# A float64 weight matrix read once, in column eighths, inside an attention loop

## The chip, the cores and the metric

The program runs on one core of one Trainium2 chip. The metric is the device time of one execution in microseconds, so lower is better; 0.3% of it is about 4.3 us.

## What is computed

Three stages follow each other: clustered attention, a feed-forward layer with a hard-swish in its middle, and a layer of eight experts with dense routing. The first matrix of the feed-forward layer is what the change is about.

```python
# q, k, v: 2 x 8 heads x 768 x 64; 16 centroids for each head; the weights come as float64
mask = q_assign[:, :, :, None] == k_assign[:, :, None, :]
scores = np.where(mask, scale * np.matmul(q, k.transpose(0, 1, 3, 2)), -1000000000.0)
attn = np.exp(scores - scores.max(-1)); attn = attn / (attn.sum(-1) + 1e-09)
x = np.matmul(attn, v)                       # to 1536 x 512
...
h = x @ w_in                                 # w_in: 512 x 2048
g = h * np.clip(h + 3.0, 0.0, 6.0) / 6.0
x = g @ w_out                                # w_out: 2048 x 512
...
out += P[:, e:e + 1] * (np.maximum(x @ w1[e], 0.0) @ w2[e])   # e = 0..7
```

## The kernel before

**The attention loop.** There are 16 heads of six blocks of 128 rows, 96 units in all. Unit g runs these steps, each for another block: `max_unit` for unit g + 8 (two small matmuls on TensorE, PE, into the one PSUM buffer `pmt`, L757; then VectorE, DVE, takes each row's maximum from it, L778), `s_mm` for unit g (eight matmuls into `pS`, L757), the exponential on ScalarE, ACT (`E`, L840), its float16 high part (`Eh`, L848) and the rest (`El`, on GpSimd, POOL, L857, or on DVE, L850), and `pv_mm` for unit g - 4 (L871). After a head's sixth maximum DVE writes the negated maxima as float16 terms to `nE` (L808 to L810), and SyncE, SP, turns them by a transposing DMA into `E` (L805). The last two matmuls of `pS` of the head's first unit need that `E`: the maxima of a head are ready at unit 6i - 2, and its first `pS` is at unit 6i.

**Preparation, beside the loop.** Heads go in pairs, counted from 0. For a pair, SP loads `qraw` and `kraw` (L477), the sum of squares goes over `red` to a scale (`qk_r`, L86, is DVE's maximum; a PE matmul, L91, spreads it to all rows), the float16 parts `nH` and `nL` are made (L624 for `nL`) and turned by transposing DMAs to `H` and `L` (L644). `sim` (PE, L655) compares with the centroids, a chain of DVE operations makes the argmax and the one-hot codes `a_oh` (L666 to L683), which a DMA turns into `ET` (L699). `abs4` (L742, L743) ends a small computation on the tile `ab`. When a head is done its output is scaled, split (`xn`, L909, POOL) and turned to `xT` (L911, SP).

**The first half of `w_in`** (512 x 1024 float64) is prepared by `first_weights` inside this loop. It goes over SP's queue twice. First, eight pieces of 512 KB (`w00x`) are read for their largest magnitude alone (L362, DVE), and one scale is made by `top_steps` (a matmul that turns the maxima, DVE's reduce, a matmul that spreads the result). Then eight column eighths of 512 KB (`w00f`, two buffers) are decoded from float64 to float32 by one ACT operation (L190) and four of DVE (L196, L198, L215, L217, `w00t`), and split into two float16 parts, `fhi` (L409, ACT) and `flo` (L412, DVE). The layer's PE work starts behind unit 95.

**What sets the order.** Everything is placed by hand: `at(unit, f)` puts a step into a unit, and tables of units (`PLACE`, `PLAN2`, `PLAN3`, `COLS`) name them; `PLAN2` holds pair 2, `PLAN3` pair 3. Each engine, and SP's queue, works in program order. A column's units in the table before are those of load, L190, the four DVE operations, `fhi` and `flo`:

```python
    COLS = [
        (44, 48, 49, 50, 61, 62, 64, 70), (45, 66, 71, 71, 72, 73, 74, 77),
        (63, 74, 78, 78, 79, 80, 81, 83), (74, 80, 84, 84, 85, 86, 87, 88),
    ] + [(u - 8, u, u + 1, u + 1, u + 2, u + 2, u + 3, u + 4) for u in (89, 95, 101, 107)]
```

Of the kernel before, what the change touches and what calls it, by code (L numbers as in the profile page):

```python
# [35 lines left out]
def attention_moe_kernel(  # L36
# [164 lines left out]

    def decode_max(m, nm):

        t = small.tile([P, 1], U32, tag="mt", name=f"{nm}_mt")
        tf = t.bitcast(F32)
        nc.vector.tensor_scalar(out=tf, in0=m, scalar1=F64_LEAST, scalar2=F64_MOST, op0=ALU.max, op1=ALU.min)
        nc.vector.tensor_scalar(
            out=t, in0=t, scalar1=5, scalar2=2, op0=ALU.logical_shift_left, op1=ALU.logical_shift_right)
        nc.vector.scalar_tensor_tensor(
            out=m.bitcast(U32), in0=m.bitcast(U32), scalar=0xC0000000, in1=t,  # L210
            op0=ALU.bitwise_and, op1=ALU.bitwise_or)
# [1749 lines left out]
```

## Time and profile before

| | us |
|---|---|
| median of 3 runs | 1437.73 (1434.11 to 1438.73) |
| the profiled execution | 1438.4, span 1436.6 |
| PE busy | 1357.0 of the span |
| DVE busy | 1169.0 |
| ACT busy | 936.9 |
| POOL busy | 839.6 |

The span is that of the profiled execution; about 1.8 us of its time lie around it. The loop's units can be found by ACT's `E` operation of each: unit 12 at 78.0 us, 24 at 106.9, 36 at 135.5, 48 at 162.7, 60 at 189.8, 72 at 221.0, 84 at 247.6 and 95 at 272.0. A busy share is a mean over the attention loop and the two layers behind it, so the rows below are read by stretch. The brackets at the end of a row of an engine's timeline give the idle time before the instruction and what ended it.

### The profile page before, as it was taken

How to read it: one execution, taken by the hardware profiler on the slowest of the kernel's cores; microseconds unless marked ns; L12 is line 12 of the kernel's file. 1: busy time of each engine (PE TensorE's matmuls, PEld its weight loads, DVE VectorE, ACT ScalarE, POOL GpSimd, SP SyncE). 2: the span in 40 equal slices, each digit the busy share in tenths (PEclk: the TensorE clock that was granted, in tenths of full speed). 3: DMA queues.
4: the chain of work that ended last, by engine and by line, in shares of the span. 5: the costliest groups of instructions: out<-in, count | busy, mean ns of one | idle time of the engine just before them, and what ended most of it. 6: DMA issues, size and time to landing. Idle time of an engine off the chain costs nothing.

```text
span 1436.6 us, 32199 instructions
## 1 busy us (share of the span) xinstructions
PE 1357.0 (94%) x12855; PEld 1049.8 (73%) x12855; DVE 1169.0 (81%) x2059; ACT 936.9 (65%) x1760; POOL 839.6 (58%) x889
## 2 busy tenths in 40 slices
PE   5779888899999988999999999999999999999998
PEld 2456655544444447878888888888888888888887
DVE  7688889677766579978997998988988988988864
ACT  5689988675563637587676566566666666656642
POOL 2588888453134448497575476466566566666631
PEclk9799999999999999999999999999999999999999
DMA  6367533323311100110201211211101111111001
GB/s 199 88 146 125 111 71 62 97 91 91 118 60 32 60 1 17 47 38 24 60 32 31 60 31 31 60 31 32 57 20 46 45 32 46 45 31 46 9 30 52
DMA packets 141399, 82.90 MB, mean 58 GB/s; under 512 B 77760, under 2 KB 137152, under 8 KB 141248
## 3 DMA queue, kind: packets, MB, share of 16 engines
q1 hardware_dynamic: 141104, 80.81, 21.3%
q8 instruction: 100, 1.64, 0.5%
q14 instruction: 51, 0.42, 0.1%
q10 hardware_dynamic: 144, 0.03, 0.0%
HBM read 64.01 MB, written 3.15 MB: 47 GB/s over the span
## 4 chain that ended last, share of the span: by engine, by line
PE 64%; DVE 18%; ACT 5%; issue 4%; POOL 4%; DMA 3%; SPq 0%; DVEq 0%; POOLq 0%; ACTq 0%
PE o_X L1771 16%; PE X L1830 16%; PE o_Z L1771 8%; PE Z L1830 8%; PE Y L1830 4%; PE o_Y L1771 4%; DVE pmt L778 4%; PE pmt L757 2%; PE pS L757 2%; PE l L1389 2%; PE pv L871 1%; DMA E<-nE 1%; DVE raw L217 1%; DVE w_t L215 1%; ACT u L1359 1%
## 5 line engine op out<-in xcount | busy, mean ns | idle before, releaser
L1830 PEld LDWEIGHTS <-wop 128*128 128x128 f16 x4032 | 394.5, 98 | 66.0 <-issue 19.1
L1771 PEld LDWEIGHTS <-g 128*128 128x128 f16 x4032 | 394.3, 98 | 46.0 <-DVE g L1735 0.4
L1771 PE MATMUL o_X<-ws,g 128*128 128x256 f16 x2304 | 312.1, 273 | 0.1
L1735 DVE TENSOR_TENSOR g<-xT,g 128x512 f16<-128x512 f32 (+1 forms) x288 | 233.6, 811 | 1.1 <-ACT g L1730 0.9
L1739 POOL TENSOR_TENSOR xT<-xT 128x256 f32<-128x256 f32 x96 | 79.3, 826 | 264.7 <-ACT xT L1841 263.9
L1830 PE MATMUL X<-xop,wop 128*128 128x256 f16 x1536 | 210.0, 274 | 11.3 <-DVE xT L1838 6.7
L857 POOL TENSOR_TENSOR El<-E,Eh 128x384 f16<-128x384 f32 x162 | 161.6, 1024 | 56.6 <-ACT Eh L848 29.5
L1730 ACT CAST g<-xT 128x512 f16<-128x512 f32 (+1 forms) x288 | 157.8, 548 | 7.4 <-POOL xT L1743 7.3
L1771 PE MATMUL o_Z<-ws,g 128*128 128x256 f16 x1152 | 156.1, 273 | 0.0
L1835 ACT COPY xT<-X 128x256 f32<-128x256 f32 x192 | 71.0, 370 | 129.4 <-PE X L1830 129.2
L1367 POOL TENSOR_TENSOR hl<-u,hh 128x512 f16<-128x512 f32 x48 | 62.1, 1294 | 88.8 <-ACT hh L1366 88.8
L1841 ACT ACTIVATE xT<-xT 128x256 f32<-128x256 f32 x192 | 100.0, 521 | 18.2 <-DVE xT L1838 17.6
L840 ACT ACTIVATE E<-pS,esc 128x768 f32<-128x768 f32 x96 | 86.4, 900 | 39.0 <-PE pS L757 28.0
L1830 PE MATMUL Z<-xop,wop 128*128 128x256 f16 x768 | 104.8, 273 | 2.6 <-ACT xT L1835 2.6
L1841 ACT ACTIVATE xT<-X 128x256 f32<-128x256 f32 x96 | 36.7, 382 | 105.1 <-PE X L1830 104.9
L1830 PE MATMUL X<-xT,wop 128*128 128x256 f16 x768 | 104.7, 273 | 0.4 <-ACT xT L1835 0.3
L1800 DVE SCALAR_TENSOR_TENSOR acc<-o_X,coef,acc 128x256 f32<-128x256 f32 x168 | 73.0, 474 | 28.0 <-PE o_X L1771 28.0
L1744 POOL TENSOR_TENSOR sb<-xT 128x256 f32<-128x256 f32 x96 | 89.4, 931 | 7.5
L1743 POOL TENSOR_TENSOR xT<-xT 128x256 f32<-128x256 f32 x96 | 92.4, 962 | 0.0
L778 DVE TENSOR_REDUCE pmt<-pmt 128x2 f32<-128x768 f32 x84 | 80.7, 960 | 12.2 <-PE pmt L757 11.2
L1740 POOL TENSOR_TENSOR sb<-xT 128x256 f32<-128x256 f32 x96 | 82.1, 855 | 6.4 <-ACT xT L1835 3.6
L1838 DVE TENSOR_TENSOR xT<-X,xT 128x256 f32<-128x256 f32 x96 | 40.2, 419 | 50.5 <-ACT g L1730 35.8
(317 smaller groups left out, 2964.7 us busy)
## 6 DMA issues: line engine op xcount, KB each, us to landing
raw<-in_moe_w_dram SPq DMA_DIRECT2D x64, 256.0 KB, 3.3
raw<-in_moe_w_dram SPq DMA_DIRECT2D x32, 512.0 KB, 3.5
w_c<-in_moe_w_out_dram SPq DMA_DIRECT2D x16, 512.0 KB, 3.3
w00x<-in_moe_w_in_dram SPq DMA_DIRECT2D x8, 512.0 KB, 4.7
w00f<-in_moe_w_in_dram SPq DMA_DIRECT2D x8, 512.0 KB, 4.7
w_c<-in_moe_w_in_dram SPq DMA_DIRECT2D x8, 512.0 KB, 4.3
vraw<-in_v_dram SPq DMA_DIRECT2D x2, 1536.0 KB, 12.8
out_dram<-acc SPq DMA_DIRECT2D x12, 256.0 KB, 2.1
```

What stands on the lines that cost most here:

```text
L778: nc.vector.tensor_reduce(nmx[i][:, 2 * j:2 * j + 2], ps[:, :, 0:N2], axis=AX.X, op=ALU.max, negate=True)
L840: nc.scalar.activation(E, ps[:, :, 0:N2], AF.Exp, scale=d["esc"][:, 0:1])
L857: nc.gpsimd.tensor_tensor(out=El[:, g], in0=E[:, g], in1=Eh[:, g], op=ALU.subtract)
L1730: nc.scalar.copy(t[:, 0] if n == 2 else t[:, 0, 0], src)
L1735: nc.vector.tensor_tensor(o, d[g], x, op=ALU.subtract)
L1739: nc.gpsimd.tensor_tensor(out=sa[:, 1], in0=q2, in1=q0, op=ALU.add)
L1740: nc.gpsimd.tensor_tensor(out=d["sb"][:, 0], in0=q3, in1=q2, op=ALU.subtract)
L1743: nc.gpsimd.tensor_tensor(out=sa[:, 0], in0=sa[:, 1], in1=q3, op=ALU.subtract)
L1744: nc.gpsimd.tensor_tensor(out=d["sb"][:, 1], in0=q1, in1=sa[:, 0], op=ALU.subtract)
L1771: nc.tensor.matmul(o, lhsT=x, rhs=r, start=first and z == 0, stop=last and z == 2, skip_group_check=True)
L1830: nc.tensor.matmul(o[n][:, 0:XT], lhsT=l, rhs=r, start=(first and c == 0 and z == 0), stop=(c == 1 and z == 2), skip_group_check=True)
L1841: nc.scalar.activation(q, q if src is None else src, AF.Relu)
```

## The change

- The scan of `w00x` is gone. Each column eighth is loaded once, as four DMAs of 128 KB (32 in all), and decoded into a tile that is kept until it is split. The largest magnitude is taken from the decoded column (`amax`).
- There are two scales, for columns 0 to 3 (units 70 to 72) and 4 to 7 (92 to 96). The second matrix half, `w01`, gets a scale of two columns that goes with them, by four small DVE operations; `half_in` and `act1` pick the scale by column.
- Decoding is spread: from unit 12 on about one DVE operation in three units, from unit 74 on about one in each. The split is at units 75 to 82 for columns 0 to 3 and at 97 to 104 for 4 to 7. A column's four loads stand in the last four units with a remainder by six of 0, 1 or 5 that are 3 to 12 units ahead of its first DVE operation.
- `abs4` of pair 0 moves from DVE to POOL. In `PLAN2` the steps from `sim` to the codes of pair 2 move from units 9 to 11 to units 11 and 12. In `PLAN3` the step that spreads pair 3's scale moves from unit 7 to unit 8.

```diff
@@ -171,6 +171,7 @@
...
+    w00, s00 = {}, {}
@@ -199,17 +200,6 @@
...
-    def decode_max(m, nm):
...
@@ -279,18 +269,31 @@
...
+            if (n, m) == (0, 1):
+                least, most = (mp.tile([P, 1], F32, name=f"w00_{x}") for x in ("least", "most"))
+                both = mp.tile([P, 2], F32, name="w01_s2")
+                nc.vector.tensor_tensor(least, s00[0], s00[1], op=ALU.min)
+                nc.vector.tensor_tensor(most, w00[0], w00[1], op=ALU.max)
+                for g in range(2):
+                    nc.vector.tensor_scalar(
+                        out=both[:, g:g + 1], in0=w00[g], scalar1=least, scalar2=d["s"], op0=ALU.mult, op1=ALU.mult)
+                wsc[0, 0], d["s"] = most, both
...
+        def sc(i):
+            k = i // 4 if (n, m) == (0, 1) else 0
+            return d["s"][:, k:k + 1]
...
@@ -346,42 +349,29 @@
         W = wsp[0, 0] = wpool.tile([P, 2, rows // P, cols], F16, tag="ws", name="w0_0_s", bufs=1)
         mx = small.tile([P, 8], F32, name="w00_mx")
...
+        def amax(f):
+            nc.vector.tensor_reduce(mx[:, f:f + 1], d["r", f], axis=AX.XY, op=ALU.max, apply_absolute_value=True)
+
+        def scale1(g, m):
+            d["s", g], w00[g] = scale_of(m, 1, TW, f"w00{g}", const)
+            s00[g] = d["s", g]
+
+        def fload(f, z):
+            part = src[P * z:P * z + P, P * f:P * f + P]
             if wide:
-                r, o = divmod(512 * i, cols)
-                part = src[P * r:P * r + P, o:o + 512].bitcast(U32)
-                d[i] = wide_tile(wdec, part, f"w00{nm}{i}", [512])
+                if z == 0:
+                    d["f", f] = wdec.tile([P, rows // P, P, 2], U32, tag="widef", name=f"w00f{f}", bufs=2)
+                nc.sync.dma_start(d["f", f][:, z].rearrange("p f t -> p (f t)"), part.bitcast(U32))
+                if z == rows // P - 1:
...
-        def amax(i):
-            c = d.pop(i)
-            x = c.bitcast(F32)[:, :, 1] if wide else c
-            nc.vector.tensor_reduce(mx[:, i:i + 1], x, axis=AX.X, op=ALU.max, apply_absolute_value=True)
-            if i + 2 < 8:
-                load(i + 2, "x")
...
-        def fload(f):
-            part = src[:, P * f:P * f + P]
-            if wide:
-                d["f", f] = wide_tile(
-                    wdec, part.bitcast(U32).rearrange("(c p) f -> p c f", p=P), f"w00f{f}", [rows // P, P], tag="widef", bufs=2)
...
         def fdec0(f):
             if wide:
-                d["t", f] = decode0(wdec, d["f", f], f"w00t{f}")
+                d["t", f] = decode0(wdec, d["f", f], f"w00t{f}", bufs=8)
...
@@ -406,20 +396,23 @@
...
         def fhi(f):
-            nc.scalar.activation(W[:, 0, :, P * f:P * f + P], d["r", f], AF.Copy, scale=d["s"])
+            nc.scalar.activation(W[:, 0, :, P * f:P * f + P], d["r", f], AF.Copy, scale=d["s", f // 4])
 
         def flo(f):
             nc.vector.scalar_tensor_tensor(
-                out=W[:, 1, :, P * f:P * f + P], in0=d.pop(("r", f)), scalar=d["s"],
+                out=W[:, 1, :, P * f:P * f + P], in0=d.pop(("r", f)), scalar=d["s", f // 4],
                 in1=W[:, 0, :, P * f:P * f + P], op0=ALU.mult, op1=ALU.subtract)
 
-        scan = [lambda: (load(0, "x"), load(1, "x"))] + [lambda i=i: amax(i) for i in range(8)]
-        scan += top_steps(lambda: mx, 2, "w00", lambda n: (ps_v.tile([P, n], F32, tag="v", name=f"w00_r{n}"), True), scale1)
-        cols_of = [
-            [lambda f=f: fload(f), lambda f=f: fdec0(f), *fdec(f), lambda f=f: fhi(f), lambda f=f: flo(f)]
+        scale = [top_steps(
+            lambda g=g: mx[:, 4 * g:4 * g + 4], 2, f"w00{g}",
+            lambda n, g=g: (ps_v.tile([P, n], F32, tag="v", name=f"w00{g}_r{n}"), True), lambda m, g=g: scale1(g, m))
+            for g in range(2)]
+        made = [
+            [*[lambda f=f, z=z: fload(f, z) for z in range(rows // P)], lambda f=f: fdec0(f), *fdec(f), lambda f=f: amax(f)]
             for f in range(8)
         ]
-        return scan, cols_of
+        split = [(lambda f=f: fhi(f), lambda f=f: flo(f)) for f in range(8)]
+        return made, scale, split
@@ -533,7 +526,7 @@
...
-    PLAN3 = [36 + n for n in [-35, -34, -30, -29, -29, -28, -26, -26, -25, -23] + PLACE[10:]]
+    PLAN3 = [36 + n for n in [-35, -34, -30, -29, -28, -28, -26, -26, -25, -23] + PLACE[10:]]
@@ -737,7 +730,7 @@
...
-            eng = nc.gpsimd if p else nc.vector
+            eng = nc.gpsimd
@@ -1059,7 +1052,7 @@
...
-    PLAN2 = [0, 1, 2, 2, 3, 3, 4, 5, 6, 7, 9, 9, 9, 10, 10, 11, 11, 18, 19, 23, 24, 25, 27]
+    PLAN2 = [0, 1, 2, 2, 3, 3, 4, 5, 6, 7, 11, 11, 11, 12, 12, 12, 12, 18, 19, 23, 24, 25, 27]
@@ -1070,15 +1063,19 @@
...
-    for n, f in zip((2, 14, 16, 20, 21, 25, 26, 30, 32, 33, 35, 36, 47, 48), wscan):
-        at(n, f)
-    COLS = [
-        (44, 48, 49, 50, 61, 62, 64, 70), (45, 66, 71, 71, 72, 73, 74, 77),
-        (63, 74, 78, 78, 79, 80, 81, 83), (74, 80, 84, 84, 85, 86, 87, 88),
-    ] + [(u - 8, u, u + 1, u + 1, u + 2, u + 2, u + 3, u + 4) for u in (89, 95, 101, 107)]
-    for units, fs in zip(COLS, wcols):
+    places = [12 * k + n for k in range(1, 6) for n in (1, 1, 2, 7)] + [
+        74, 75, 76, 77, 79, 80, 81, 82, 83, 85, 86, 87, 88, 88, 89, 90, 90, 91, 91, 92]
+    for f, fs in enumerate(wmade):
+        u = places[5 * f:5 * f + 5]
+        first = [n for n in range(u[0] - 12, u[0] - 2) if n % 6 in (0, 1, 5)][-4:]
+        for n, g in zip(first + [u[0] - 1] + u, fs):
+            at(n, g)
+    for units, fs in zip(((70, 71, 71, 72, 72), (92, 93, 93, 95, 96)), wscale):
         for n, f in zip(units, fs):
             at(n, f)
+    for n, fs in zip((75, 77, 79, 81, 97, 99, 101, 103), wsplit):
+        for o, f in enumerate(fs):
+            at(n + o, f)
@@ -1190,8 +1187,9 @@
...
-        iv = mp2.tile([P, 1], F32, tag="hinv", name=f"hinv{n}")
-        nc.vector.tensor_tensor(iv, wsc[n, 0], sv[1], op=ALU.mult)
+        iv = mp2.tile([P, 2], F32, tag="hinv", name=f"hinv{n}")
+        for g in range(2):
+            nc.vector.tensor_tensor(iv[:, g:g + 1], w00[g] if n == 0 else wsc[n, 0], sv[1], op=ALU.mult)
@@ -1356,7 +1354,7 @@
...
-        nc.scalar.activation(u, p1, AF.Relu, bias=three[:, 0:1], scale=cfac[n, "in"][:, 0:1])
+        nc.scalar.activation(u, p1, AF.Relu, bias=three[:, 0:1], scale=cfac[n, "in"][:, f // 4:f // 4 + 1])
```

From the attention loop on, lines are seven lower in the changed kernel (L805 becomes L798, L778 becomes L771); the decode's L215 and L217 are there L205 and L207, the loads L364.

**DVE, units 6 to 8.** Before; the operations on `ab` and `Wt` are `abs4` of pair 0, `nL` with `kraw` and `qk_r` belong to the next pairs:

```order
L778 TENSOR_REDUCE pmt<-pmt 128x2
L624 SCALAR_TENSOR_TENSOR nL_400<-qraw_222,qk_s_544,nH_614 128x768
L778 TENSOR_REDUCE pmt<-pmt 128x2
L742 TENSOR_TENSOR ab_656<-ab_656,Wt_95 16x64
L743 TENSOR_TENSOR Wt_95<-ab_656 16x64
L742 TENSOR_TENSOR ab_656<-ab_656,Wt_95 16x64
L743 TENSOR_TENSOR Wt_95<-ab_656 16x64
L624 SCALAR_TENSOR_TENSOR nL_400<-kraw_225,qk_s_544,nH_614 128x768
L86 TENSOR_REDUCE qk_r<-red_704 128x1
L778 TENSOR_REDUCE pmt<-pmt 128x2
```

After:

```order
L771 TENSOR_REDUCE pmt<-pmt 128x2
L617 SCALAR_TENSOR_TENSOR nL_400<-qraw_222,qk_s_542,nH_612 128x768
L771 TENSOR_REDUCE pmt<-pmt 128x2
L617 SCALAR_TENSOR_TENSOR nL_400<-kraw_225,qk_s_542,nH_612 128x768
L86 TENSOR_REDUCE qk_r<-red_704 128x1
L771 TENSOR_REDUCE pmt<-pmt 128x2
```

The four operations between two `pmt` reduces are gone from DVE, so `nL` and `qk_r` follow the reduce at once.

**SP's queue around unit 66.** `E_11` are the maxima of head 11, needed at unit 66. Before:

```order
L911 DMA_TRANSPOSE xT<-xn_3471 128x6x128
L184 DMA w00f_3771<-in_moe_w_in_dram 128x4x256
L805 DMA_TRANSPOSE E_11_3780<-nE_94 128x3x128
L911 DMA_TRANSPOSE xT<-xn_3767 128x6x128
L805 DMA_TRANSPOSE E_12_4096<-nE_93 128x3x128
```

After:

```order
L904 DMA_TRANSPOSE xT<-xn_3464 128x6x128
L798 DMA_TRANSPOSE E_11_3772<-nE_94 128x3x128
L364 DMA w00f_3857<-in_moe_w_in_dram 128x256 x3
L904 DMA_TRANSPOSE xT<-xn_3761 128x6x128
L798 DMA_TRANSPOSE E_12_4090<-nE_93 128x3x128
```

The load of a column now stands behind that transpose, not ahead of it, and as three smaller ones.

**SP's queue around unit 84.** `E_14` is needed there; the brackets name the semaphores that an instruction waits for. Before (`w00f_4654` is column 4, `w00f_4926` column 5):

```order
L911 DMA_TRANSPOSE xT<-xn_4380 128x6x128 [waits DMAHW0_49,Activation_49,Pool_49]
L184 DMA w00f_4654<-in_moe_w_in_dram 128x4x256 [waits DMAHW1_49,DVE_49]
L805 DMA_TRANSPOSE E_14_4663<-nE_94 128x3x128 [waits DMAHW2_49,DVE_49,PE_49]
L911 DMA_TRANSPOSE xT<-xn_4649 128x6x128 [waits DMAHW3_49,Activation_49,Pool_49]
L184 DMA w00f_4926<-in_moe_w_in_dram 128x4x256 [waits DMAHW5_49,DMAHW4_49,DVE_49]
L805 DMA_TRANSPOSE E_15_4931<-nE_94 128x3x128 [waits DVE_49,PE_49]
```

After (`w00f_4172` is column 5, `w00f_4484` column 6, `w00f_4572` column 7):

```order
L364 DMA w00f_4172<-in_moe_w_in_dram 128x256 [waits DMAHW3_49]
L364 DMA w00f_4484<-in_moe_w_in_dram 128x256 [waits DMAHW4_49,DVE_49,Activation_49]
L364 DMA w00f_4484<-in_moe_w_in_dram 128x256 [waits DMAHW5_49]
L364 DMA w00f_4484<-in_moe_w_in_dram 128x256 [waits DMAHW6_49]
L364 DMA w00f_4572<-in_moe_w_in_dram 128x256 [waits DMAHW3_49,DMAHW0_49,DMAHW7_49,DVE_49,Activation_49]
L904 DMA_TRANSPOSE xT<-xn_4385 128x6x128 [waits Pool_49]
L798 DMA_TRANSPOSE E_14_4680<-nE_94 128x3x128 [waits DMAHW1_49,PE_49]
L364 DMA w00f_4484<-in_moe_w_in_dram 128x256 [waits DMAHW2_49]
L364 DMA w00f_4572<-in_moe_w_in_dram 128x256
```

The first load of column 7 stands ahead of `xT` and `E_14`, and waits for DVE: column 7 takes the buffer of column 5, whose last decode operation is in unit 83.

## Rows read from the trace of the kernel before

**Rows 1.** The page: busy time, share of the span and instructions of each engine.

```profile
PE 1357.0 (94%) x12855; PEld 1049.8 (73%) x12855; DVE 1169.0 (81%) x2059; ACT 936.9 (65%) x1760; POOL 839.6 (58%) x889
```

**Rows 2.** Stretches: length; busy PE, PEld, DVE, ACT, POOL; PE's clock; DMA; GB/s.

```profile
78.00:106.90 28.90, 23.98 (x441) 16.49 (x437) 25.73 (x48) 25.15 (x37) 28.31 (x34) 1.00 0.76 162
106.90:135.50 28.60, 25.80 (x453) 17.59 (x451) 24.05 (x46) 25.76 (x40) 21.79 (x28) 0.94 0.70 121
135.50:162.70 27.20, 23.98 (x434) 16.54 (x431) 23.08 (x44) 24.86 (x38) 23.83 (x29) 1.00 0.76 139
162.70:189.80 27.10, 24.21 (x451) 17.05 (x447) 25.43 (x53) 25.49 (x39) 23.98 (x29) 1.00 0.36 64
189.80:221.00 31.20, 24.71 (x422) 16.83 (x419) 24.87 (x40) 23.85 (x34) 25.82 (x30) 0.95 0.33 71
221.00:247.60 26.60, 22.89 (x401) 15.72 (x400) 25.42 (x38) 23.75 (x34) 23.06 (x26) 1.00 0.41 79
262.00:288.00 26.00, 26.00 (x311) 15.04 (x310) 17.87 (x30) 14.79 (x21) 7.58 (x8) 0.94 0.41 112
61.60:67.00 5.40, 5.38 (x44) 2.95 (x44) 3.31 (x7) 1.73 (x2) 2.17 (x3) 0.50 0.74 149
206.60:210.40 3.80, 3.72 (x39) 2.14 (x39) 1.62 (x4) 2.31 (x4) 2.74 (x4) 0.55 0.00 0
```

**Rows 3.** Waits, 30 to 262 us: us in total, times, longest.

```profile
PE pmt L757 <- DVE pmt L778: 14.4, 27, 1.3
```

**Rows 4.** Timeline of PE: start, us, instruction, idle before it and its end.

```profile
61.62 0.58 PE L91 MATMUL red<-ident,qk_r 128*128 128x2 f32 x2 [3.87 <-DVE qk_r L86]
69.62 0.47 PE L655 MATMUL sim<-CT,L 128*128 128x32 f16 x12 [0.76 <-DMA L<-nL]
106.47 0.34 PE L757 MATMUL pS<-E,ET 64*128 64x384 f16 x2 [2.31 <-DMA E<-nE]
206.68 0.34 PE L757 MATMUL pS<-E,ET 64*128 64x384 f16 x2 [3.48 <-DMA E<-nE]
261.79 0.51 PE L757 MATMUL pS<-E,ET 64*128 64x384 f16 x2 [2.57 <-DMA E<-nE]
```

**Rows 5.** Groups of DVE, 57 to 61 us: count, busy us, mean ns, idle before.

```profile
L742 DVE TENSOR_TENSOR ab<-ab,Wt 16x64 f32<-16x64 f32 x2 | 1.7, 840 | 0.0
L743 DVE TENSOR_TENSOR Wt<-ab 16x64 f16<-16x64 f32 x2 | 1.2, 586 | 0.1
```

**Rows 6.** Timeline of SP's queue: start, us, issue.

```profile
199.20 1.21 SPq L911 DMA_TRANSPOSE xT<-xn  x1
200.50 0.53 SPq L184 DMA_DIRECT2D w00f<-in_moe_w_in_dram  x1
```

**Rows 7.** The chain that ended last: start, us, what.

```profile
201.13 5.51 DMA E<-nE
```

**Rows 8.** Tile E: time from a DMA's issue to its landing.

```profile
DMA to landing us min/median/max: 2.3/3.8/5.5
```

**Rows 9.** Groups of DVE, 60 to 130 us.

```profile
L362 DVE TENSOR_REDUCE w_mx<-w00x 128x1 f32<-128x512 f32 x8 | 5.4, 674 | 0.0
```

**Rows 10.** Groups of DVE, 160 to 262 us.

```profile
L196 DVE TENSOR_SCALAR w00t<-w00t 128x512 f32<-128x512 f32 x4 | 3.7, 928 | 0.0
L198 DVE TENSOR_SCALAR w00t<-w00t 128x512 uint32<-128x512 uint32 x4 | 3.7, 922 | 0.1
L215 DVE SCALAR_TENSOR_TENSOR w00t<-w00f,w00t 128x512 uint32<-128x512 uint32 x4 | 4.9, 1220 | 0.0
L217 DVE SCALAR_TENSOR_TENSOR w00t<-w00f,w00t 128x512 uint32<-128x512 uint32 x4 | 5.0, 1241 | 0.0
L412 DVE SCALAR_TENSOR_TENSOR w_s<-w00t,w_s,w_s 128x512 f16<-128x512 f32 x4 | 3.3, 821 | 0.0
```

**Rows 11.** Tile w00t: shortest, median, longest ns of one, first and last start.

```profile
L217 DVE SCALAR_TENSOR_TENSOR w00t<-w00f,w00t x8: 691/1038/1403, 194.4 to 286.9; 128x512 uint32<-128x512 uint32 x8
```

**Rows 12.** Tile w_r, the chain of the one scale before.

```profile
L81 PE MATMUL w_r<-ident,pad x1: 305/305/305, 133.7 to 133.7; 128*128 128x128 f32 x1
```

More of the change, by code (lines that the diff above doesn't have):

```diff
@@ L200, in decode1 @@
         ]
-    def decode_max(m, nm):
[L204 to L211, printed above, removed]
     def decode2(c, t, dst):
@@ L285, in scale1 @@
                 wsp[n, m] = wsbuf[:, n].rearrange("p (z a f) -> p z a f", z=2, f=cols)
+        def sc(i):
+            k = i // 4 if (n, m) == (0, 1) else 0
+            return d["s"][:, k:k + 1]
         def hi(i):
-            nc.scalar.activation(view(wsp[n, m][:, 0], i), view(d["raw"], i), AF.Copy, scale=d["s"][:, 0:1])
+            nc.scalar.activation(view(wsp[n, m][:, 0], i), view(d["raw"], i), AF.Copy, scale=sc(i))
         def lo(i):
@@ L292, in lo @@
             nc.vector.scalar_tensor_tensor(
-                out=view(wsp[n, m][:, 1], i), in0=view(d["raw"], i), scalar=d["s"][:, 0:1],
+                out=view(wsp[n, m][:, 1], i), in0=view(d["raw"], i), scalar=sc(i),
                 in1=view(wsp[n, m][:, 0], i), op0=ALU.mult, op1=ALU.subtract)
@@ L347, in first_weights @@
         mx = small.tile([P, 8], F32, name="w00_mx")
-        def load(i, nm):
-            if wide:
-                r, o = divmod(512 * i, cols)
-                part = src[P * r:P * r + P, o:o + 512].bitcast(U32)
-                d[i] = wide_tile(wdec, part, f"w00{nm}{i}", [512])
-            else:
-                d[i] = wdec.tile([P, 512], F32, tag="wide", name=f"w00{nm}{i}", bufs=2)
-                r, o = divmod(512 * i, cols)
-                nc.sync.dma_start(d[i], src[P * r:P * r + P, o:o + 512])
@@ L359, in amax @@
-        def amax(i):
-            c = d.pop(i)
-            x = c.bitcast(F32)[:, :, 1] if wide else c
-            nc.vector.tensor_reduce(mx[:, i:i + 1], x, axis=AX.X, op=ALU.max, apply_absolute_value=True)
-            if i + 2 < 8:
-                load(i + 2, "x")
-        def scale1(m):
-            m1 = small.tile([P, 1], F32, name="w00_m1")
-            nc.vector.tensor_copy(m1, m)
-            if wide:
-                decode_max(m1, "w00")
-            d["s"], wsc[0, 0] = scale_of(m1, 1, TW, "w00", const)
@@ L373, in fload @@
-        def fload(f):
-            part = src[:, P * f:P * f + P]
-            if wide:
-                d["f", f] = wide_tile(
-                    wdec, part.bitcast(U32).rearrange("(c p) f -> p c f", p=P), f"w00f{f}", [rows // P, P], tag="widef", bufs=2)
-            else:
-                t = d["f", f] = wdec.tile([P, rows // P, P], F32, tag="widef", name=f"w00f{f}", bufs=2)
-                nc.sync.dma_start(t, part.rearrange("(c p) f -> p c f", p=P))
+        def amax(f):
+            nc.vector.tensor_reduce(mx[:, f:f + 1], d["r", f], axis=AX.XY, op=ALU.max, apply_absolute_value=True)
@@ new lines, in scale1 @@
+        def scale1(g, m):
[3 more added lines that the diff above has]
+            part = src[P * z:P * z + P, P * f:P * f + P]
+            if wide:
+                if z == 0:
+                    d["f", f] = wdec.tile([P, rows // P, P, 2], U32, tag="widef", name=f"w00f{f}", bufs=2)
+                nc.sync.dma_start(d["f", f][:, z].rearrange("p f t -> p (f t)"), part.bitcast(U32))
+                if z == rows // P - 1:
+                    d["f", f] = d["f", f].rearrange("p a f t -> p (a f) t")
+            else:
+                if z == 0:
+                    d["f", f] = wdec.tile([P, rows // P, P], F32, tag="widef", name=f"w00f{f}", bufs=8)
+                nc.sync.dma_start(d["f", f][:, z], part)
@@ L944, in scan_v @@
             AF.Square, accum_out=vmx[:, n:n + 1])
-    wscan, wcols = first_weights()
+    wmade, wscale, wsplit = first_weights()
     first0, main0, last0 = prep_tasks(0)
```

## Prediction

> **What bounds the kernel now.** I read the page's busy line first [rows 1]: TensorE (PE) is busy for 94% of the span, VectorE (DVE) for 81%. That mean hides two stages, so the next view is the busy time by stretch [rows 2]. From 262 us on PE is busy 26.00 of 26.00 us: whatever is done beside it there is free. Before that, in the attention loop of 96 units, PE is busy only 23 to 26 us in a stretch of twelve units, which takes 26.6 to 31.2 us, and DVE is busy 23.1 to 25.7 us of them, POOL as much as 28.31 of 28.90 in units 12 to 23. No engine is full in the loop as a whole: it is a lockstep. PE fills the one `pmt` buffer, DVE reduces it, PE may fill it again; the summed waits of the loop name this pair, 14.4 us in 27 waits [rows 3]. The long waits are few and stand in PE's own timeline [rows 4]: 3.87 us at 61.6 for `qk_r`, and 2.31, 3.48 and 2.57 us at units 24, 66 and 90 for the transposed row maxima `E`, which SP's queue delivers. After a long stall PE also runs for a while at half its clock: 0.50 granted over 61.60 to 67.00, 0.55 over 206.60 to 210.40, the lower of the two levels, 1.2 GHz [rows 2]. So the loop pays for three things: DVE's work between two `pmt` reduces, late transposes, and the slow clock behind them. The change touches all three.
>
> **Units 7 to 16.** Four small DVE operations on `ab` and `Wt` (`abs4` of the first pair) go to POOL: 1.7 + 1.2 = 2.9 us [rows 5]. They stand ahead of `nL` and the `qk_r` reduce that PE awaits for 3.87 us, so that wait shrinks to about 1.0; the consumer is also moved one unit later (unit 7 to 8), which covers the rest. Behind it 5.38 us of PE work ran at half clock, where it would take 2.7 at full: 2.7 more to gain. Against that, `sim` of the third pair, two units later now, still waits for `L` (0.76 us now, [rows 4]), since three of the new loads stand between the loads of `kraw` and `L`'s transpose; and its chain of argmax operations on DVE falls between the `pmt` reduces of units 11 to 14 instead of 9 to 11. POOL takes the four operations at a cost that I bound by DVE's own 2.9 us; who waits for it there is the subtraction of `El`, which PE needs four units later. All gained would be -3.87 - 2.7 = -6.6; if the argmax chain and POOL give most of it back, -2. I take **-4**, since the stall itself has its cause removed and the clock follows the stall.
>
> **Transposes without a load ahead.** The eight 512 KB scan loads are gone, the eight 512 KB column loads become 32 loads of 128 KB. Before, SP's rows at unit 66 read `xT` 1.21 us and a 512 KB load 0.53 [rows 6], then `E`, which lands 5.51 us after its issue [rows 7], against a median of 3.8 for all fifteen [rows 8]. Afterwards the load stands behind `E` at units 24, 66 and 90: `E` is issued 0.6 earlier and may land up to 1.7 sooner, 2.3 in all at unit 66 of a stall of 3.48, with part of the half clock (3.72 us of PE work at 0.55, some 1.7 lost). But at unit 66 three loads come right behind `E`, and may slow it as the load ahead did. I take -2 (-4 to -0.6). Unit 24 likewise -2 (-3.6 to -0.6) of a stall of 2.31; at unit 90 only the issue is earlier, -0.6 (-1.2 to 0). Sum **-4.6**.
>
> **Decode work drawn into the loop.** Before, four columns are decoded in the loop and the last four from about unit 89 on, most of it where PE is full. Now seven columns and a half are decoded before unit 91, and `amax` reads each decoded column instead of the raw piece (0.67 us [rows 9], taken as the same). One column's four operations in the loop cost 0.93 + 0.92 + 1.22 + 1.24 = 4.31 us, its `flo` 0.82 [rows 10]. By the units of the two tables the change of DVE's work is: units 12 to 35, a column, its `amax` and three operations of the next, 8.05, against eight scans of 0.67, 5.4: +2.7; units 36 to 59, 7.8 against 1.85, +6.0; units 60 to 71, 4.05 against 5.1, -1.1; units 72 to 83, two columns, an amax and four `flo`, 12.6 against 8.4, +4.2; units 84 to 87, 2.5 against 4.3, -1.8. That is +10.0 us. How much of it reaches the time? DVE idles 3.2, 4.6, 4.1, 1.7, 6.3 and 1.2 us in the six stretches from unit 12 to 83 [rows 2]. Units 48 to 59 carry 2.35 us more DVE work than units 36 to 47 and take no longer (27.1 against 27.2), so in the slack stretches I let a quarter through: 0.25 x 8.7 = 2.2. Units 72 to 83 have 1.2 us to spare for 4.2: 3.0 goes through. The relieved stretches return half of 2.9: -1.5. Sum **+3.7** (0 to +10.0). ACT gets at most two more casts of a column in units 72 to 83, about the 0.82 of their DVE twin each, and has 2.85 us idle there: nothing, at worst +1.6.
>
> The stretched forms are plain in the trace: `L217` takes from 0.69 to 1.40 us on one shape [rows 11], the short ones behind the loop, where POOL is busy for 7.58 of 26.00 us [rows 2]. The Trainium skill (Advanced Engine Details and Errata, "Mode Summary") says that the Vector engine's second SBUF port is shared with GPSIMD, so that the two block each other's instructions. By that rule every decode operation in the loop would take its long form, about 13% over the mean, 0.56 us for each of six columns, and my sum would be some 2 us higher (1442); the trace's loop mean of 1.24 says that not all do.
>
> **One transpose held on the queue.** The order of SP's instructions shows a wait that was not there. The columns use two buffers in turn, so the first load of column 7 waits for the last decode operation of column 5, at unit 83; it is issued in program order ahead of `xT` and of the `E` transpose for unit 84, whose maxima are ready at unit 82. Before, a load stood ahead of it too, but that one waited for a column finished at unit 80 and let `E` go in time: no wait of PE stands at unit 84. PE wants that `E` at unit 84, just about when DVE ends unit 83's decode: then come the load 0.53, `xT` 1.21 and the landing 3.8 (2.3 to 5.5) [rows 6, 8], a stall of 5.6 (4.1 to 7.3). The two stalls nearest in size were followed by half clock [rows 2]: the 1.7 of unit 66 here too. The other engines catch up meanwhile, and I take off one wait of 1.3, the longest between PE and the reduce [rows 3]. Sum **+6.0** (+3 to +9).
>
> **Small.** The second scale brings one more chain of a transposing matmul, a DVE reduce and a spreading pair of matmuls into units 93 to 95, where PE is full: three float32 matmuls of about 0.3 us [rows 12], **+0.8**. Four columns' worth of decode less after unit 92, and 4.2 MB less to load: 0, as PE is full there [rows 2].
>
> **Sum.** -4 - 4.6 + 3.7 + 6.0 + 0.8 = +1.9 on the profiled run's 1438.4 us, 1440.3; that run lies 0.7 above the median of 1437.73, so about **1440** (1439.6) for the median.
>
> **The rivals.**
> 1. *DVE is the bound of the loop* (slower). Then all +10.0 us of its added work reaches the time instead of 3.7: 1440 + 6.3 = 1446. For it: the most frequent wait of the loop is PE's for DVE's `pmt` reduce, and in units 72 to 83 DVE is busy for 25.42 of 26.60 us. Against it: the equal spans of units 36 to 47 and 48 to 59. It decides if the idle of DVE in units 12 to 59 cannot be used, because it sits behind single stalls and not between the reduces. Chance 0.28.
> 2. *The held transpose costs little* (faster). If DVE runs ahead of PE by then, because the stalls before were PE's, the decode of unit 83 ends early, the load goes out in time and +6.0 falls away: 1434. Against it: in the order PE's unit 84 is one `pmt` reduce behind that decode, and PE has but one `pmt` buffer. Chance 0.14.
> 3. *The early stalls go wholly* (faster): -6.6 instead of -4 at unit 7, and the whole 2.31 + 3.48 + 2.57 = 8.4 instead of 4.6 at the three transposes: 1440 - 6.4 = 1434. For it: each of these stalls has one cause that the trace names. Against it: in a lockstep the next wait is seldom far; `sim` already waits 0.76 behind the first one. Chance 0.13.
> 4. *The change doesn't do what it says.* The order shows 32 loads, no scan and the new waits: no chance worth a number.
>
> **How the numbers follow.** My forecast, gains of 8.6 against costs of 10.5, has 0.45: 1436 to 1443 by itself. The bounds of the terms are wide and of both signs; rivals 2 and 3 give 1434, rival 1 1446; the range **1432 to 1448** leaves out only the cases in which two of them go the same way. 0.3%, 4.3 us, is about what a measurement of this kernel can tell from no change. Faster by more than that: rivals 2 and 3 mostly, with the low end of mine, 0.25; slower: rival 1, with a held transpose of over 8 us, 0.30; within, 0.45.
>
> **What would show it.** After the change, PE's wait for `qk_r` should be gone or under 1 us and the clock near 62 to 67 us full; the `E` waits at units 24 and 66 under 1 and 2 us; at unit 84 a new wait of PE for `E` of 4 to 7 us, with a row of about half clock behind it, and SP's first load of column 7 going out only behind DVE's last decode of column 5; units 72 to 83 some 3 us longer and units 36 to 59 1 to 2 us longer; from unit 95 on no difference but a shift. I am wrong if the wait at unit 84 is missing or under 2 us, if units 36 to 59 lengthen by 5 us, or if the stretch after unit 95 changes in length by more than 2 us.

## The result and the profile after

The changed kernel takes 1444.78 us (median of 6 runs, 1443.75 to 1446.44) against 1436.95 us before (6 runs): a ratio of 1.006, 95% interval 1.0046 to 1.0074, so 7.8 us slower. Its profiled run took 1445.28 us with a span of 1443.5, 6.9 more than before's span.

The page of after, to be read against [rows 1]: PE's work is the same to 0.2 us, DVE's is 9 us more.

```profile
PE 1356.8 (94%) x12858; PEld 1051.8 (73%) x12858; DVE 1178.1 (82%) x2063; ACT 935.8 (65%) x1760; POOL 842.0 (58%) x893
```

Stretches of twelve units in after, from unit 12 to unit 83, columns as in [rows 2]:

```profile
69.33:102.64 33.31, 25.36 (x437) 17.45 (x437) 29.15 (x49) 26.39 (x41) 27.37 (x35) 0.95 0.47 101
102.64:131.34 28.70, 24.30 (x451) 17.19 (x447) 26.43 (x49) 25.96 (x41) 23.55 (x29) 1.00 0.47 102
131.34:159.76 28.42, 23.98 (x439) 16.96 (x435) 26.11 (x47) 25.47 (x40) 23.78 (x29) 1.00 0.54 105
159.76:187.79 28.03, 23.88 (x438) 16.78 (x435) 26.57 (x47) 25.37 (x39) 24.69 (x29) 1.00 0.41 72
187.79:216.36 28.57, 23.23 (x425) 16.14 (x422) 25.34 (x42) 22.46 (x33) 24.39 (x29) 1.00 0.37 87
216.36:250.40 34.04, 23.06 (x402) 15.63 (x399) 27.96 (x46) 25.00 (x38) 26.13 (x28) 0.95 0.27 57
```

Their lengths against before: 33.31 (28.90), 28.70 (28.55), 28.42 (27.26), 28.03 (27.10), 28.57 (31.23), 34.04 (26.55). Units 36 to 59 are 2.1 us longer together, units 60 to 71 2.7 shorter, units 72 to 83 7.5 longer. The first of the six is longer since unit 12 begins 8.7 us sooner and the argmax chain behind it is done later.

What is left of [rows 4] in PE's timeline of after, with what came in its place:

```profile
72.95 0.48 PE L750 MATMUL pmt<-H 64*128 64x384 f16 x2 [3.67 <-DVE a_oh L676]
245.13 0.34 PE L750 MATMUL pmt<-H 64*128 64x384 f16 x2 [2.00 <-DVE pmt L771]
249.80 0.50 PE L750 MATMUL pS<-E,ET 64*128 64x384 f16 x2 [3.68 <-DMA E<-nE]
262.42 0.34 PE L750 MATMUL pS<-E,ET 64*128 64x384 f16 x2 [0.53 <-DMA E<-nE]
271.50 0.48 PE L81 MATMUL w_r<-ident,pad 128*128 128x128 f32 x1 [2.57 <-DVE pad L105]
```

The wait for `qk_r` is gone, and `E` is awaited at unit 84 for 3.68 us and at unit 90 for 0.53, no more at units 24 and 66. In their place PE waits 3.67 us for the argmax chain at unit 12, 2.00 us for DVE's reduce just ahead of unit 84, and 2.57 us at 271.50 for the maximum that opens the second scale. The summed wait of PE for DVE's reduce (30 to 262 us) doubled, from 14.4 us in [rows 3]:

```profile
PE pmt L750 <- DVE pmt L771: 27.9, 30, 3.0
```

PE's granted clock (the first number behind the five engines) was full where it had been half, at 60 to 66 us, and half at 271.5 to 277 (0.71 on the mean of 249.8 to 257.0):

```profile
60.00:66.00 6.00, 5.04 (x87) 3.29 (x84) 5.06 (x14) 4.86 (x7) 5.63 (x11) 1.00 1.10 242
249.80:257.00 7.20, 7.20 (x92) 4.28 (x91) 3.76 (x5) 5.16 (x7) 3.86 (x7) 0.71 0.27 76
271.50:277.00 5.50, 5.50 (x55) 3.26 (x56) 1.98 (x5) 2.77 (x4) 2.54 (x3) 0.50 0.08 18
```

### The profile page after: what moved, and what is told of

Its sections match the earlier page's. It is cut to its first block, busy times and chain, and to the rows that moved or that the text cites. A ratio compares the mean times of both kernels' runs of the same rounds, so it can differ in the third digit from the quotient of the medians.

```text
span 1443.5 us, 32244 instructions
## 1 busy us (share of the span) xinstructions
PE 1356.8 (94%) x12858; PEld 1051.8 (73%) x12858; DVE 1178.1 (82%) x2063; ACT 935.8 (65%) x1760; POOL 842.0 (58%) x893
## 4 chain that ended last, share of the span: by engine, by line
PE 71%; DVE 7%; POOL 6%; ACT 4%; issue 4%; DMA 1%; DVEq 0%; SPq 0%; POOLq 0%; ACTq 0%
PE o_X L1769 16%; PE X L1828 16%; PE o_Z L1769 8%; PE Z L1828 8%; PE l L1387 6%; PE Y L1828 4%; PE o_Y L1769 4%; PE l L1038 3%; PE l L1040 3%; PE l L1039 3%; POOL El L850 2%; DVE pmt L771 1%; ACT E L833 1%; POOL wop L1550 1%; PE pS L750 1%
## 5 line engine op out<-in xcount | busy, mean ns | idle before, releaser
L771 DVE TENSOR_REDUCE pmt<-pmt 128x2 f32<-128x768 f32 x84 | 80.7, 960 | 13.8 <-PE pmt L750 12.8
```

The costliest lines, as they stand in the source:

```text
L771: nc.vector.tensor_reduce(nmx[i][:, 2 * j:2 * j + 2], ps[:, :, 0:N2], axis=AX.X, op=ALU.max, negate=True)
```

## The experiments

All ratios are against runs of the kernel before on the same chip; differences between two changed kernels are taken from their ratios. Stretches are compared by ACT's `E` operation of a unit.

| kernel | us (median) | ratio, 95% interval |
|---|---|---|
| changed | 1444.78 | 1.0060 (1.0046 to 1.0074) |
| e1, load of column 7 later | 1438.81 | 1.0023 (1.0013 to 1.0032) |
| e2, second scale's chain later | 1442.13 | 1.0037 (1.0024 to 1.0051) |
| e3, both | 1437.99 | 1.0011 (1.0002 to 1.0020) |
| e4, before with the early part | 1433.39 | 0.9984 (0.9975 to 0.9993) |
| e5, before with loads behind `E` | 1434.44 | 0.9986 (0.9977 to 0.9995) |
| e6, e4 and e5 | 1428.25 | 0.9949 (0.9936 to 0.9963) |
| e7, before with more DVE work | 1440.64 | 1.0028 (1.0017 to 1.0040) |
| e8, no second scale | 1445.64 | 1.0061 (1.0048 to 1.0074) |
| e9, no decode of columns 0 to 3 | 1435.38 | 0.9997 (0.9988 to 1.0005) |
| e10, e1 without decode of 4 and 5 | 1434.48 | 0.9988 (0.9979 to 0.9997) |
| e11, e1 without second scale | 1438.34 | 1.0011 (1.0001 to 1.0020) |
| e12, e6 with small loads | 1429.60 | 0.9957 (0.9941 to 0.9972) |

### The held transpose: e1

```diff
+        if f == 7:
+            first = [84, 84, 85, 85]
         for n, g in zip(first + [u[0] - 1] + u, fs):
```

> The changed kernel with the four loads of column 7 at units 84 and 85, behind the transpose of E for unit 84 instead of ahead of it; nothing else moves. Theory (a held transpose): PE's wait of 3.7 us for E at unit 84 and the half clock behind it go, some 5 us less than the changed kernel: about 1440. Rival (VectorE is the bound there, the transpose only shows it): the same time is waited for the pmt reduce, 1443 or more.

The theory held: 1.0023 against 1.0060, so 0.37%, 5.3 us, are gone, known to some 2.4. In after the maxima are written at 240.08, but column 5's last decode operation only starts at 244.98 (timeline of DVE); the load goes out at 245.73 and `E` at 247.42 (SP's queue); it lands 2.33 us later (chain that ended last):

```profile
240.08 0.18 DVE L803 SCALAR_TENSOR_TENSOR nE<-pmt,nE 128x6 f16<-128x6 f32 x1
244.98 0.68 DVE L207 SCALAR_TENSOR_TENSOR w00t<-w00f,w00t 128x512 uint32<-128x512 uint32 x1
```

```profile
245.73 0.33 SPq L364 DMA_DIRECT2D w00f<-in_moe_w_in_dram  x1
246.10 1.22 SPq L904 DMA_TRANSPOSE xT<-xn  x1
247.42 1.19 SPq L798 DMA_TRANSPOSE E<-nE  x1
```

```profile
247.42 2.33 DMA E<-nE
```

In e1 the same stretch, units 72 to 83, is 30.03 us long instead of 34.04, though the four units behind it still run at a mean clock of 0.82; PE no longer waits for `E`, but still 2.00 us for DVE's reduce, as in after, so that wait is no part of the held transpose:

```profile
218.09:248.12 30.03, 22.73 (x404) 15.55 (x402) 27.71 (x46) 25.01 (x38) 25.13 (x27) 1.00 0.30 61
248.12:257.60 9.48, 9.48 (x152) 6.10 (x151) 7.00 (x8) 7.18 (x9) 7.40 (x12) 0.82 0.28 79
```

```profile
246.87 0.34 PE L750 MATMUL pmt<-H 64*128 64x384 f16 x2 [2.00 <-DVE pmt L771]
```

### The second scale: e2, e3, e8, e11

The chain two units later, alone and with e1's edit:

```diff
-    for units, fs in zip(((70, 71, 71, 72, 72), (92, 93, 93, 95, 96)), wscale):
+    for units, fs in zip(((70, 71, 71, 72, 72), (93, 95, 95, 96, 96)), wscale):
```

> The changed kernel with the second scale's steps at units 93, 95, 95, 96, 96 instead of 92, 93, 93, 95, 96, so that PE's turning matmul stands two units later. Theory (a matmul queued ahead of VectorE's decode): PE's wait of 2.6 us at 271 us and most of the half clock behind it go, 3 to 4 us less than the changed kernel: about 1441. Rival (VectorE's decode of column 7 is late for PE in any place): PE waits as long two units later, 1444 to 1445.

> Both edits of the two runs before together. Theory (two separate waits): the gains add, 8 to 9 us less than the changed kernel, about 1436, level with the kernel before. Rival (VectorE is the bound from unit 72 to the loop's end): whatever one wait gives back the next takes, 1441 or more.

Both moves together come to 1.0011, 7.0 us less than the changed kernel; the chain alone is worth 0.23% (3.3 us) in e2 and 0.12% (1.7 us) between e1 and e3. These differences are known to some 2 to 3 us, so the gains add within what can be told, and the 1.7 alone is not clear of nothing. PE still waits in e3, two units later, for what holds the buffer of the turned maxima, 2.35 us, so part of the wait only moved:

```profile
268.09 0.30 PE L81 MATMUL w_r<-ident,pad 128*128 128x128 f32 x1 [2.35 <-DVE x_f L894]
```

In the profiles of e1 and e2 this matmul waits not at all and 0.16 us, but there PE had just lost 3.88 and 3.72 us to the `E` of unit 90, where after and e3 lose 0.53 and 0.52. The two waits can hide each other, so these pairs of kernels don't price the chain alone.

Then the chain was left out altogether, from the changed kernel and from e1:

```diff
-    for units, fs in zip(((70, 71, 71, 72, 72), (92, 93, 93, 95, 96)), wscale):
+    for units, fs in zip(((70, 71, 71, 72, 72),), wscale):
...
             d["s", g], w00[g] = scale_of(m, 1, TW, f"w00{g}", const)
             s00[g] = d["s", g]
+            d["s", 1], w00[1], s00[1] = d["s", g], w00[g], s00[g]
```

> The changed kernel without the second scale's own steps: columns 4 to 7 are split with the first scale, so the turning and spreading matmuls, the reduces and the four scale operations of units 92 to 96 are left out. Theory (the chain puts PE behind VectorE's decode of column 7, a wait of 2.6 us and a half clock): 4 to 5 us less than the changed kernel, about 1440. The forecast's price of it was 0.8: 1444.

> The changed kernel with column 7's loads at units 84 and 85 and without the second scale's own steps (left out: turning, spreading and scale operations of units 92 to 96; columns 4 to 7 use the first scale). Theory (the chain's wait is a cost of its own beside the held transpose): 3 us or more less than the kernel with the loads moved alone, 1435 to 1436. Rival (PE's wait for VectorE there is taken elsewhere, as the time without the chain suggested): the same as with the loads moved alone, 1438 to 1439.

By the times the expectation fell: 1.0061, nothing gained, and in e11 1.7 us. The one profile of each shows that they differ in another place too. Their transposes of `L` land some half a microsecond later, though no instruction near them was changed, and PE waits for `L` at 69.95 us in e8 (2.39 us at 68.99 in e11), which it doesn't in after. Tile `L` from issue to landing in after, e8 and e11, and PE's row in e8:

```profile
DMA to landing us min/median/max: 3.2/3.6/5.2
```

```profile
DMA to landing us min/median/max: 3.7/4.2/5.6
```

```profile
DMA to landing us min/median/max: 3.7/4.1/5.6
```

```profile
69.95 0.49 PE L649 MATMUL sim<-CT,L 128*128 128x32 f16 x12 [2.38 <-DMA L<-nL]
```

Unit 24 is 3.9 us later in e8 than in after, 2.4 of it by this wait. Behind it, from unit 90 to the first matmul of the layer (278.6 us in after, unit 90 at 264.46), e8 needs 4.8 us less than after. So the chain's wait is there in the trace and goes with the chain, and the late `L` can hide its gain; but its worth in time is not settled: 3.3, 1.7, 1.7 and 0 us by four pairs of kernels. Why the transposes land later in these two kernels is open.

### The gains alone: e4, e5, e6

e4 is the kernel before with `abs4`, `PLAN2` and `PLAN3` of the change; e5 has three loads behind the transposes; e6 has both.

```diff
-            eng = nc.gpsimd if p else nc.vector
+            eng = nc.gpsimd
...
-    PLAN2 = [0, 1, 2, 2, 3, 3, 4, 5, 6, 7, 9, 9, 9, 10, 10, 11, 11, 18, 19, 23, 24, 25, 27]
+    PLAN2 = [0, 1, 2, 2, 3, 3, 4, 5, 6, 7, 11, 11, 11, 12, 12, 12, 12, 18, 19, 23, 24, 25, 27]
...
-    for n, f in zip((2, 14, 16, 20, 21, 25, 26, 30, 32, 33, 35, 36, 47, 48), wscan):
+    for n, f in zip((2, 14, 16, 20, 23, 25, 26, 30, 32, 33, 35, 36, 47, 48), wscan):
...
-        (63, 74, 78, 78, 79, 80, 81, 83), (74, 80, 84, 84, 85, 86, 87, 88),
-    ] + [(u - 8, u, u + 1, u + 1, u + 2, u + 2, u + 3, u + 4) for u in (89, 95, 101, 107)]
+        (65, 74, 78, 78, 79, 80, 81, 83), (74, 80, 84, 84, 85, 86, 87, 88),
+    ] + [(u - 8 + 2 * (u == 95), u, u + 1, u + 1, u + 2, u + 2, u + 3, u + 4) for u in (89, 95, 101, 107)]
```

> The kernel before with only the first pair's abs4 on POOL, the third pair's sim to codes two units later and the fourth pair's scale one unit later. Theory: PE's wait of 3.9 us and the half clock behind it go, the argmax chain takes some back: 4 us less than before, about 1433. Rival (what the early units gain the lockstep fills again by unit 24): 1436 to 1437.

> The kernel before with three of its 512 KB loads behind the transposes of E for units 24, 66 and 90 instead of ahead of them. Theory (each stall has the load as its cause): the waits of 2.3, 3.5 and 2.6 us go in part, and some half clock with them: 4 to 5 us less than before, 1432 to 1433. Rival (lockstep: PE waits for VectorE's reduce instead, or the transposes are as late without the load): within 1 us of before.

> The kernel before with the edits of the two runs before together, no other decode. Theory: the gains add, 8 to 9 us less than before, about 1428 to 1429. Rival: they are the same slack of VectorE seen twice, no more than the larger one alone, about 1432.

Alone they gave 2.3 and 2.0 us (each known to 1.3), half of what was expected; together 7.3 us (known to 1.9), nearly what was expected of the two. In e5's profile the gain of unit 24 (2.1 us) is lost again to a wait for `E` at unit 30, which was 0.31 us in before (2.20 in e4, 1.43 in e6):

```profile
119.01 0.50 PE L757 MATMUL pS<-E,ET 64*128 64x384 f16 x2 [2.33 <-DMA E<-nE]
```

Together they give 3.0 us more than the two alone, just beyond what these intervals can tell. e6 is the fastest kernel of the study and beats both others: it keeps the scan and both loads, and only moves work off the waits.

### How much of DVE's work reaches the time: e7, e9, e10

e7 adds nine operations on an unused tile to the kernel before; e9 leaves the four decode operations of columns 0 to 3 out of the changed kernel, e10 those of columns 4 and 5 out of e1.

```diff
+    for n in (37, 37, 38, 43, 49, 49, 50, 55, 56):
+        at(n, lambda: nc.vector.tensor_scalar(out=dums, in0=dums, scalar1=0.0, scalar2=None, op0=ALU.add))
```

For e9 (in e10 the columns are 4 and 5):

```diff
-                    parts.pop(0)()
+                    g = parts.pop(0)
+                    if f not in (0, 1, 2, 3):
+                        g()
```

> The kernel before with nine more VectorE operations of a column's size (128x512 float32, on a tile that nothing reads) in units 37 to 56, the places of the change's decode; at the 0.93 us of such an operation in the loop some 8.4 us of VectorE work. Theory (a quarter of it reaches the time): about 2 us more than before. Rival (VectorE is the bound of the loop): 6 to 8 us more.

> The changed kernel with the four VectorE decode operations of columns 0 to 3 left out (units 13 to 62, some 17 us of VectorE work; loads, casts, largest magnitudes and splits stay). Theory (a part of the decode beside the loop reaches the time; 3.3 us came back between units 24 and 63): 4 us less than the changed kernel or somewhat more, about 1440. Rival (the stretches there are set by other waits): less than 1.5 us. Rival (VectorE is the bound): 8 us or more, 1436.

> The kernel with column 7's loads at units 84 and 85, with the VectorE decode operations of columns 4 and 5 left out (units 74 to 83, 8.6 us of VectorE work). Theory (units 75 to 81 lose 3.3 to 3.5 us to them): 3 to 4 us less than that kernel, about 1435. Rival (slack taken up elsewhere): within 1 us of it, 1438 to 1439.

The tile of e7 (shortest, median, longest ns of one):

```profile
L1085 DVE TENSOR_SCALAR dums<-dums x9: 415/1081/1141, 136.0 to 184.1; 128x512 f32<-128x512 f32 x9
```

What e9 leaves out, as it stands in after (69 to 200 us: count, busy us, mean ns, idle before):

```profile
L197 DVE TENSOR_SCALAR w00t<-w00t 128x512 f32<-128x512 f32 x4 | 2.3, 580 | 0.0
L199 DVE TENSOR_SCALAR w00t<-w00t 128x512 uint32<-128x512 uint32 x4 | 4.4, 1106 | 0.0
L205 DVE SCALAR_TENSOR_TENSOR w00t<-w00f,w00t 128x512 uint32<-128x512 uint32 x4 | 5.1, 1272 | 0.0
L207 DVE SCALAR_TENSOR_TENSOR w00t<-w00f,w00t 128x512 uint32<-128x512 uint32 x4 | 4.7, 1165 | 0.0
```

What e10 leaves out, as it stands in e1 (218 to 248 us), with the four `flo` there, which stay:

```profile
L197 DVE TENSOR_SCALAR w00t<-w00t 128x512 f32<-128x512 f32 x2 | 1.3, 672 | 0.0
L199 DVE TENSOR_SCALAR w00t<-w00t 128x512 uint32<-128x512 uint32 x2 | 2.3, 1134 | 0.0
L205 DVE SCALAR_TENSOR_TENSOR w00t<-w00f,w00t 128x512 uint32<-128x512 uint32 x2 | 1.5, 751 | 0.0
L207 DVE SCALAR_TENSOR_TENSOR w00t<-w00f,w00t 128x512 uint32<-128x512 uint32 x2 | 1.4, 682 | 0.0
L402 DVE SCALAR_TENSOR_TENSOR w_s<-w00t,w_s,w_s 128x512 f16<-128x512 f32 x4 | 4.9, 1221 | 0.0
```

The nine operations of e7 took 8.0 us in its trace and cost 0.28%, 4.0 us: 50%. e9 takes 16.5 us away and gains 0.63% on the changed kernel, 9.0 us: 55%. e10 takes 6.5 us away, not the 8.6 reckoned ahead, and gains 0.35% on e1, 5.0 us: 77%. The intervals of the ratios leave these shares open by some 21, 15 and 29 points to either side. So in units 12 to 62 about a half of DVE's work reaches the time, neither the quarter of the prediction nor the whole of rival 1; in units 74 to 83, where DVE has little idle, more does, and there the whole is not excluded.

PE's summed wait for the reduce (30 to 262 us) in e7 and in e9, against 14.4 in before and 27.9 in after:

```profile
PE pmt L757 <- DVE pmt L778: 19.4, 27, 1.6
```

```profile
PE pmt L752 <- DVE pmt L773: 20.2, 25, 2.0
```

The cost of all the moved decode, without the held transpose, is e3 or e11 against e6, 0.62%, 8.9 us, known to 2.3 (in e3 some 2 of it is still the second scale's: from unit 90 to the layer's first matmul e3 needs 2.0 us more than e8; in e11 2.4 is the wait for `L`). By stretch, units 12 to 83 of e6, to be read against after's rows above:

```profile
69.84:101.45 31.61, 25.19 (x437) 17.21 (x437) 27.24 (x49) 25.84 (x40) 26.98 (x35) 0.95 0.65 136
101.45:129.42 27.97, 24.32 (x449) 16.98 (x446) 26.44 (x50) 25.80 (x41) 23.52 (x29) 1.00 0.84 146
129.42:156.73 27.31, 23.95 (x434) 16.52 (x431) 23.31 (x45) 25.02 (x39) 24.20 (x30) 1.00 0.76 139
156.73:183.54 26.81, 24.31 (x453) 17.12 (x450) 25.20 (x50) 25.49 (x39) 23.57 (x29) 1.00 0.36 64
183.54:212.75 29.21, 23.20 (x422) 16.37 (x420) 25.24 (x40) 23.53 (x34) 25.84 (x30) 1.00 0.35 75
212.75:239.47 26.72, 22.84 (x401) 15.67 (x399) 25.32 (x38) 23.75 (x34) 23.20 (x26) 1.00 0.36 78
```

After (and, in the last stretch, e1) needs 1.7, 0.7, 1.1, 1.2, -0.6 and 3.3 us more than e6: 7.4 us in sum. The first of these is 1.1 by e3's profile and 2.6 by e1's, so it is the least certain. PE's summed wait for the reduce, in e6 and in e3:

```profile
PE pmt L757 <- DVE pmt L778: 16.1, 28, 1.7
```

```profile
PE pmt L750 <- DVE pmt L771: 30.0, 35, 3.0
```

### Smaller loads: e12

e12 issues each 512 KB load of e6 as four of 128 KB in the same place, as here for a column:

```diff
+                for z in range(rows // P):
+                    nc.sync.dma_start(
+                        t[:, z].rearrange("p f t -> p (f t)"), src[P * z:P * z + P, P * f:P * f + P].bitcast(U32))
```

> The kernel before with the early edits and the loads behind the transposes, and each 512 KB load issued as four of 128 KB in the same place. Theory (what delays a transpose is a load ahead of it, not its size): the same as with the 512 KB loads, 1428 within 2 us. Rival (small loads let a transpose land sooner): 2 to 4 us less. Rival (three more issues for each load hold up the queue): 2 us or more above.

1429.60 against 1428.25, 0.08% or 1.1 us by the ratios, known to 2.9: the size of the loads makes no difference that can be told. A gain of 2 us or more is excluded, a cost of that size is not.

## Why the prediction was right or wrong

It said 1440 with a range of 1432 to 1448, most likely no change that can be told (0.45), and slower as the likelier side (0.30). The time lies in the range, 4.8 us above the forecast, and slower came. It is near rival 1's 1446, but not by rival 1's sum: the held transpose and the early gains are in both, and the decode costs about 7 us, not 10. Point by point:

| term | forecast, us | measured, us |
|---|---|---|
| units 7 to 16, and transposes without a load ahead | -4 - 4.6 = -8.6 | -7.3 (e6; -2.3 and -2.0 alone, e4 and e5) |
| decode work in the loop | +3.7 | about +7 (e3 against e6, 8.9, less some 2 of the second scale's wait; 7.4 in units 12 to 83) |
| the held transpose | +6.0 | +5.3 (after against e1) |
| second scale | +0.8 | 0 to +3.3 (after to e2 or e8; e1 to e3 or e11) |

- **The step that failed** is the share of DVE's added work in units 12 to 59. "In the slack stretches I let a quarter through" put 2.2 us in for 8.7 of work; against e6 these units are 1.7, 0.7, 1.1 and 1.2 us longer, 4.8 in sum, and e7 and e9 let 50 and 55% through. The time went into PE's wait for the reduces: 14.4 us in before, 19.4 with e7's added work, 27.9 in after, 20.2 without the decode of columns 0 to 3. The change did not take the slack away together with the stalls of [rows 4]: e6 has lost those at `qk_r` and at units 24, 66 and 90 and waits only 1.7 us more for the reduces than before, and e7 keeps them and still loses a half. That idle summed over twelve units doesn't tell how much of it lies between two reduces, where an added operation has to fit, is how I read these waits; what is shown is the share.
- **Two spans that are equal are poor evidence for free work.** The quarter rested on units 36 to 47 and 48 to 59 of before, 27.2 and 27.1 us with 2.35 us more DVE work in the second. The first held an `E` stall that the second did not; it was put in no account. Without it the first would be some 25.6 us (an estimate: 27.26 less 1.69), and the same two spans would have shown 1.5 of 2.35 us going through. PE's row in before:

```profile
149.63 0.34 PE L757 MATMUL pS<-E,ET 64*128 64x384 f16 x2 [1.69 <-DMA E<-nE]
```

- **Units 72 to 83** came out near the forecast: +3.0 was worked out from 1.2 us of idle and 4.2 of work, +3.3 measured (e1 against e6). In part that is luck: the two columns' decode took 6.5 us there and not 8.6, the four `flo` 4.9 and not 3.3.
- **The held transpose** was right in place and cause, and near in size: the order of SP's queue gave it, and e1 gives back 5.3 us of the 6.0. PE's own wait, 3.68 us, is under the 4 to 7 that were named and the 5.6 that were reckoned. Inside the sum two sizes were off: the landing took 2.33 us and not 3.8, and the clock of 0.71 over the 7.2 us behind the wait is some 2.1 us lost (an estimate) where I had put 1.7. How much of the low clock is the wait's is not clear, since e1 shows 0.82 in units 84 to 87 without it.
- **The early part** was right in its cause. The `qk_r` wait went whole, the clock at 60 to 66 us was full, unit 12 came 8.7 us sooner, and the argmax chain took 4.6 of that back by unit 15. Some of the rest is not the change's: e5 and e7 have before's code up to there, and their profiles reach unit 16 1.9 and 2.3 us sooner than before's. From unit 6 to unit 16 before, e5 and e7 need 30.5, 30.0 and 30.4 us, after and e4 27.0, so 3.0 to 3.5 for the 4 forecast; in the time e4 is worth 2.3. The transposes were put at 4.6 and give 2.0 alone. That the two come to 7.3 together, near the forecast's 8.6, is in part luck, since neither alone came near its own term.
- **The second scale** was priced by its own matmuls. What counts is what PE waits for at the first of them: DVE's decode of column 7, queued ahead of the reduce, 2.57 us in the trace, and half clock behind it. Its worth in time stays open between 0 and 3.3 us.
- **The rule of the Trainium skill** (Advanced Engine Details and Errata, "Mode Summary": DVE's second port is shared with GPSIMD) gave 1442, nearer to the time, but not for its reason. In e7 at least five of nine equal operations took 1.08 us or more, and the shortest 0.415: not all took the long form, as in before. In e1's units 72 to 83 `L199` took 1.13 us, `L205` and `L207` 0.75 and 0.68. (The 13% in that sum is `L217`'s alone.)
- **Behind unit 95** the prediction's own sign of being wrong, a change of over 2 us, came true: ACT's `E` of unit 95 comes 3.9 us later (272.02 and 275.96), the end 6.9, so the stretch is 3.0 longer. Most of it lies ahead of the layer, whose first matmuls come 6.1 us later: there PE still ran at half clock behind the second scale's wait, until about 277 us. From those matmuls on 0.8 us are left.

## What to carry to other kernels

In a loop in which two engines hand one buffer to and fro, price work on the second engine at half its duration or more until a test says otherwise (50, 55 and 77% here); idle time summed over a stretch is no measure of what fits between two hand-overs. Two equal spans are a test only when both hold the same stalls. Before a load is put ahead on an in-order queue, ask which buffer it takes over and who reads that last: everything behind it on the queue inherits that wait. A repair that only moves (e1, e6) may be worth more than the saving that came with it: 4.2 MB less to read gave nothing that a run here shows by itself.

## What was not expected of the hardware

The transposing DMA of `E` (same shape, fifteen times) lands after 3.8 us in the median of before [rows 8], and after 2.3 us in the median of the changed kernel (3.0 in e7's profile, whose queue has the order of before):

```profile
DMA to landing us min/median/max: 2.3/2.3/2.9
```

One and the same transpose, for unit 90, with nothing else issued on SP's queue for some 9 us ahead of it but `xT`, took 4.62 us in the profile of e1 (chain that ended last) and 4.56 in e2's, while e3, with the same order there as e1, issued it at 253.92 us and had PE wait for it only 0.52, until 256.28 (timeline of PE):

```profile
258.43 4.62 DMA E<-nE
```

```profile
256.28 0.34 PE L750 MATMUL pS<-E,ET 64*128 64x384 f16 x2 [0.52 <-DMA E<-nE]
```

A wait of 3.9 us with half clock behind it (0.50 over 263.09 to 268.00 in e1) comes and goes with that, and single runs of e1 range from 1437.4 to 1442.3 us, of e3 from 1434.6 to 1439.3. That this wait makes up these ranges is not shown. What decides it was not found.
